# Linear attention with a squared-ReLU gate on one core: q rest formed with k and transposed by DMA, 1/den repeated through DRAM, g tiles on 128 rows, last tile in column parts

## Chip, cores and metric

One core of a Trainium2 chip. The metric is device microseconds of one execution; medians of several executions are quoted with their range. "Before" is the kernel without the change. Names of groups such as "k", "h", "g" are explained below.

## The reference

bf16 inputs, one batch of S = 2048 tokens, D = 448 features, F = 1792 hidden features, H = 16 heads of Dh = 28.

```python
def attention(x):                       # x here is LN(x)
    q, k, v = split(x @ wqkv)           # 16 heads of 28 each
    phi = lambda t: where(t > 0, t + 1, exp(t)) + 1e-6
    kv  = einsum("bhsd,bhse->bhde", phi(k), v)
    z   = einsum("bhsd->bhd", phi(k))
    num = einsum("bhqd,bhde->bhqe", phi(q), kv)
    den = einsum("bhqd,bhd->bhq", phi(q), z) + 1e-6
    return merge_heads(num / den) @ wo

def mlp(x):                             # again LN(x)
    r = relu(x @ w1 + b1)
    return (r * r) @ w2 + b2

xn  = layernorm(x)
out = x + attention(xn) * silu(mlp(xn))
```

## The kernel before

The kernel orders its own instructions. A Python description adds operations with the tiles that they read and write; the order on TensorE (PE) and on the DMA-issuing SyncE (SP) is the order of the description, and a list scheduler reorders ScalarE (ACT), VectorE (DVE) and GpSimd (POOL).

The stages on PE are: **k** (16 tiles of 128 tokens), **q** (4 groups of 512 tokens by 3 blocks of 128 features), **q rest** (the last 64 of 448 q features), **h** (x·w_1), then the **token sums** A = xnᵀ·phi(k), from which two small products (**fold_wv**, **fold_wo**) make one 448x448 matrix msb; **z** and **den**; the **spread** of 1/den over features; **g** (h²·w_2, 16 tiles), and **s** (scaled phi(q)·msb, 16 tiles). K = 448 is 3.5 times 128, so most products run as two 64-row halves of the array at once, one for each of two tiles, in seven half steps. `phase` is the function that interleaves two tiles; `half[0]` and `half[1]` are rows 0 to 63 and 64 to 127.

k and q rest, before:

```python
def kk(si):
    b = Buf("K")
    def mm(e, h, c, start, stop):
        return e.matmul(ps(b)[:, 0:D], xT[half[h], c, si*P:(si+1)*P], w_qkv[half[h], c, D:2*D], ...)
    return Acc(b, [("xT", si)] + wnames("wk"), mm, lambda: phi(b, pk[:, si, :], ("pk", si), P, D), D)

def q_rest(pair):                       # 64 features, two groups of 512 tokens side by side in columns
    b = Buf("Q")
    def mm(e, h, c, start, stop):
        for i in (0, 1):
            g = 2*pair + i
            last = e.matmul(ps(b)[half[i], 0:512], w_qkv[half[h], c, 384:448],
                            xT[half[h], c, g*512:(g+1)*512], ...)
        return last
    ...
```

1/den, before: `rden` is a [128, 512] tile with one row for each head and token group. A selector matrix `ehd` repeats each row over the 28 features of its head, into PSUM, and DVE multiplies phi(q) by it:

```python
def spread(*what):                      # seven calls, two (group, feature block) each
    bufs = [Buf("RB") for _ in what]
    def f(e, _):
        for h, (g, r) in enumerate(what):
            w = ehd[half[h], g % 2, r*P:(r+1)*P] if r < 3 else ehr[half[h], :, :]
            last = e.matmul(ps(bufs[h])[:, 0:512], w, rden[half[h], :], start=True, stop=True)
        return last
    add("pe", f, ["rden", "ehd", "ehr"], bufs, 0.22)
    for (g, r), b in zip(what, bufs):   # 14 products on DVE, one operand in PSUM
        ...  e.tensor_tensor(out=sl, in0=sl, in1=ps(b)[:, 0:512], op=ALU.mult)
```

The order after the last h group, and the last tile, before (cut):

```python
r0, r1 = q_rest(0), q_rest(1)
phase((r0, K4), (r1, K4)); phase((r1, K3), (r0, K3))
token_sum(0); z_heads(); token_sum(1); den(); token_sum(2); token_sum(3); fold_wv()
...                                     # six h tiles and the first g pairs, with spread() between them
gd = gg(15, True)                       # last g tile, a 64-row half beside s tiles, bias by matmul
...
ss_columns(15, 0)                       # last s tile: two halves of 224 columns,
ss_columns(15, 1)                       # each 3 matmuls on 128 rows and 1 on 64
```

Of the kernel before, what the change touches and what calls it, by code (L numbers as in the profile page):

```python
# [9 lines left out]
P = 128  # L10
# [270 lines left out]
def bass_recurrent_scan__linear_attn_block__dense_activation_squared_relu__prompt_kernel(  # L281
    nc, A_x, A_wqkv, A_wo, B_x, B_w1, B_b1, B_w2, B_b2, out
):
    with ExitStack() as es:
# [11 lines left out]
        c64 = sb("c64", [P, P], bf)  # L296
        ones = sb("ones", [P, 1], bf)
        ehd = sb("ehd", [P, 2, D], bf)
        ehr = sb("ehr", [P, 2, 64], bf)
# [15 lines left out]
        pqR = sb("pqR", [P, 2, 512], bf)  # L315
        pk = sb("pk", [P, NT, D], bf)
        zacc = sb("zacc", [P, D], f32)
        zb = sb("zb", [P, D], bf)
        at = sb("at", [P, 4, D], bf)
        r2 = sb("r2", [P, NF, S], bf)  # L320
        kvm = sb("kvm", [P, 4, D], bf)
        msb = sb("msb", [P, 4, D], bf)
        zsb = sb("zsb", [P, 5, 32], bf)
# [3 lines left out]
        obuf = sb("obuf", [P, 8, D], bf)  # L327
        pbank = [es.enter_context(nc.psum_tensor(f"pb{i}", [P, 512], f32)) for i in range(PSUM_BANKS)]

# [36 lines left out]
        pool(lambda e, _: e.memset(ones[:, :], 1.0), ["ones"], dur=0.1)  # L366
        pool(lambda e, _: e.memset(zmask[:, :, :], 1.0), ["zmask"])
# [5 lines left out]
        def late_constants(gate):  # L373
            pool(lambda e, _: e.memset(kvm[:, :, :], 0.0), ["kvm"], gate, dur=1.6)
            pool(lambda e, _: e.memset(hmask[:, :], 1.0), ["hmask"], gate)
            band("hmask", hmask[:, :].rearrange("p (b j) -> p b j", b=HC), [[-DH, HC], [0, DH]], 0)
            pool(lambda e, _: e.memset(ehd[:, :, :], 0.0), ["ehd"], gate, dur=0.85)  # L377
            for g in range(NG):
                ev = ehd[:, g % 2, :].rearrange("p (b j) -> p b j", b=NH)
                pool(  # L380
                    lambda e, _, g=g, ev=ev: e.affine_select(
                        out=ev, in_=ev, pattern=[[-1, NH], [0, DH]], compare_op=ALU.not_equal, fill=1.0,
                        base=-32 * g, channel_multiplier=1,
                    ),
                    ["ehd"], ["ehd"], dur=0.7,
                )
            pool(lambda e, _: e.tensor_copy(ehr[:, :, :], ehd[:, :, 384:448]), ["ehr"], ["ehd"])
            pool(lambda e, _: e.memset(c64[:, :], 1.0 / 64), ["c64"], gate)
# [35 lines left out]
        load_k("sp", w_qkv, A_wqkv, "wk", D, 2 * D)  # L424
# [5 lines left out]
        load_k("sp", w_qkv, A_wqkv, "wq", 0, D)  # L430
# [143 lines left out]
        def phi(buf, slot, tile, rows, n):  # L574

            act_d = 0.544 if n == D else 0.6
            add(
                "act", lambda e, _: e.activation(out=slot, in_=ps(buf)[0:rows, 0:n], func=AF.Exp), [buf, "actw"],  # L578
                [tile], act_d,
            )  # L580
            add(
                "dve",
                lambda e, _: e.tensor_scalar(
                    out=slot, in0=slot, scalar1=1.0, scalar2=1e-6, op0=ALU.min, op1=ALU.add
                ),
                [tile], [tile], 0.25,
            )
            add(
                "dve",
                lambda e, _: e.scalar_tensor_tensor(  # L590
                    out=slot, in0=ps(buf)[0:rows, 0:n], scalar=1.0 + 1e-6, in1=slot, op0=ALU.add, op1=ALU.max
                ),
                [tile, buf], [tile], 0.625 if n == D else 0.69,
            )

        def kk(si):
            b = Buf("K")

            def mm(e, h, c, start, stop):
                return e.matmul(  # L600
                    ps(b)[:, 0:D], xT[half[h], c, si * P : (si + 1) * P], w_qkv[half[h], c, D : 2 * D], start=start,
                    stop=stop,
                )

            return Acc(b, [("xT", si)] + wnames("wk"), mm, lambda: phi(b, pk[:, si, :], ("pk", si), P, D), D)

        def zsum(i):
# [5 lines left out]
                    out=o[:, :], in0=pk[:, 0, :] if i == 1 else zacc[:, :], in1=pk[:, i, :], op=ALU.add  # L613
                ),
                [("pk", i), ("pk", 0) if i == 1 else "zacc"], ["zb" if i == NT - 1 else "zacc"], 0.55,
            )

        def qq(g, m):
# [9 lines left out]
            return Acc(b, reads, mm, lambda: phi(b, pqT[:, m, g * 512 : (g + 1) * 512], ("pq", g, m), P, 512), 512)  # L628

        def q_rest(pair):  # L630

            b = Buf("Q")

            def mm(e, h, c, start, stop):
                for i in (0, 1):
                    g = 2 * pair + i
                    last = e.matmul(  # L637
                        ps(b)[half[i], 0:512], w_qkv[half[h], c, 384:448], xT[half[h], c, g * 512 : (g + 1) * 512],
                        start=start, stop=stop,
                    )  # L640
                return last

            reads = [("xT", 8 * pair + i) for i in range(8)] + wnames("wq")
            return Acc(b, reads, mm, lambda: phi(b, pqR[:, pair, :], ("pqr", pair), P, 512), 512)
# [29 lines left out]
        def token_sum(c):  # L674
# [3 lines left out]
            def f(e, _):  # L678
                last = None
                for si in range(NT):  # L680
                    if c < 3:
                        last = e.matmul(  # L682
                            ps(b)[:, 0:D], xn[:, si, c * P : (c + 1) * P], pk[:, si, :], start=(si == 0),
                            stop=(si == NT - 1),
                        )
                    else:
                        r = slice(64 * (si % 2), 64 * (si % 2) + 64)
                        last = e.matmul(  # L688
                            ps(b)[r, 0:D], xn[:, si, 384:448], pk[:, si, :], start=(si < 2), stop=(si >= NT - 2)
# [14 lines left out]
        def z_heads():  # L704
# [3 lines left out]
            def f(e, _):  # L708
                for r in range(3):
                    e.matmul(  # L710
                        ps(b)[:, r : r + 1], zb[:, r * P : (r + 1) * P], ones[:, :], start=(r == 0), stop=True,
                        skip_group_check=True,
                    )
                for col in (3, 4):
                    for i in (0, 1):
                        last = e.matmul(
                            ps(b)[half[i], col : col + 1], zb[:, 384:448], ones[:, :], start=False, stop=True,
                            skip_group_check=True,
                        )
                return last  # L720
# [10 lines left out]
        def fold_wv():  # L731
# [20 lines left out]
            def mask(e, _):  # L752
                o = kvm[0:PD, 0, 0:PD]
                o = bass.AP(tensor=o.tensor, offset=o.offset, ap=[o.ap[0], [D + PD, 4], [1, PD]])
# [5 lines left out]
            add("dve", mask, [b, "hmask"], ["kvm"], 0.65)  # L760

        def fold_wo(r):
# [3 lines left out]
            def f(e, _):  # L766
                if r == 3:
                    for i in (0, 1):
                        last = e.matmul(
                            ps(b)[half[i], 0:D], kvm[0:PD, 3, 384:448], w_o[0:PD, 3, :], start=True, stop=True  # L770
                        )
                    return last
# [17 lines left out]
            to(msb[:, r, :], half[2], [("msb", r)])  # L790
        denb = Buf("DEN")

        def den():
            def f(e, _):
                last = None
                for c in range(4):
                    for g in range(NG):
                        if c < 3:
                            z, q = zsb[:, c, :], pqT[:, c, g * 512 : (g + 1) * 512]
                        else:  # L800
                            z, q = zsb[:, 3 + g % 2, :], pqR[:, g // 2, :]
                        last = e.matmul(  # L802
                            ps(denb)[32 * g : 32 * g + 32, 0:512], z, q, start=(c == 0), stop=(c == 3)
# [4 lines left out]
                "pe", f, ["zsb", ("pqr", 0), ("pqr", 1)] + [("pq", g, c) for g in range(NG) for c in range(3)], [denb],  # L808
                4 * 0.24,
# [11 lines left out]
        def spread(*what):  # L821


            bufs = [Buf("RB") for _ in what]

            def f(e, _):
                for h, (g, r) in enumerate(what):
                    w = ehd[half[h], g % 2, r * P : (r + 1) * P] if r < 3 else ehr[half[h], :, :]
                    last = e.matmul(ps(bufs[h])[:, 0:512], w, rden[half[h], :], start=True, stop=True)  # L829
                return last  # L830

            add("pe", f, ["rden", "ehd", "ehr"], bufs, 0.22)
            for (g, r), b in zip(what, bufs):
                sl = pqT[:, r, g * 512 : (g + 1) * 512] if r < 3 else pqR[:, g // 2, :]
                name = ("pq", g, r) if r < 3 else ("pqr", g // 2)
                add(
                    "dve",
                    lambda e, _, sl=sl, b=b: e.tensor_tensor(out=sl, in0=sl, in1=ps(b)[:, 0:512], op=ALU.mult),  # L838
                    [b, name], [name], 0.68,
                )  # L840

        first_g = [True]

        def gg(si, last=False):

            b = Buf("G")

            def mm(e, h, fi, start, stop):
                if fi == NF:
                    return e.matmul(ps(b)[:, 0:D], c64[half[h], :], b2b[half[h], :], start=start, stop=stop)  # L850
                return e.matmul(  # L851
                    ps(b)[:, 0:D], r2[half[h], fi, si * P : (si + 1) * P], w_2[half[h], fi, :], start=start, stop=stop
                )

            def out():
                gs = gbuf[:, si % 8, :]
                if not last:
                    add(
                        "dve", lambda e, _: e.tensor_tensor(out=gs, in0=ps(b)[:, 0:D], in1=b2b[:, :], op=ALU.add),  # L859
                        [b, "b2b"], [("g", si % 8)], 0.624,  # L860
                    )
                if first_g[0]:
                    first_g[0] = False
                    add(
# [258 lines left out]
```

## Time and profile before

| | before |
|---|---|
| median of 3 runs | 147.03 us (147.02 to 147.06) |
| span of the profiled run | 145.9 us |
| PE busy | 140.8 us (97%) |
| DVE, ACT, POOL busy | 97.2, 79.8, 21.2 us |
| first h matmul starts | 9.80 us |
| first h to last matmul start | 132.88 us |
| last matmul start to end of span | 3.18 us |

The last rows are worked out from the matmul start times in the trace.

The head of the page of before: busy microseconds, share of the span and instruction count of each engine.

```profile
span 145.9 us, 3228 instructions
...
PE 140.8 (97%) x1330; PEld 69.1 (47%) x1330; DVE 97.2 (67%) x224; ACT 79.8 (55%) x154; POOL 21.2 (15%) x39
```

A row of the table of stretches of before, 80 to 90 us: for each stretch, its length and the busy time of each engine, then the granted clock, the DMA share and GB/s.

```profile
core 0: us, PE busy (x) PEld busy (x) DVE busy (x) ACT busy (x) POOL busy (x), PEclk, DMA share, GB/s
...
80.00:90.00 10.00, 10.00 (x98) 4.86 (x96) 6.41 (x12) 4.43 (x8) 0.00 (x0) 1.00 0.01 2
```

PE is busy 10.00 of 10 us, DVE and ACT less; the same holds for every stretch from 10 to 140 us, but for 9.93 at 60 to 70. So a microsecond of PE work removed is a microsecond of time, as long as no new wait replaces it. What PE does between 64 and 100 us is in the chain of waits, cut here to that stretch (start, duration, what; "x16" is a run of 16 matmuls):

```profile
66.22 1.02 PE pb L637 x16
67.28 0.84 PE pb L637 x12
68.12 3.13 PE pb L682 x16
...
81.39 0.97 PE pb L650 x8
82.36 0.22 PE pb L829 x2
82.57 1.51 PE pb L650 x14
```

L637 is q rest, L682 the token sums, L650 h, L829 the spread. They follow each other with hardly a gap. The groups of instructions that the change touches, with count, busy us, mean ns of one, and idle time before them with what ended it:

```profile
L838 DVE TENSOR_TENSOR pqT<-pqT,pb 128x512 bf16<-128x512 bf16 x12 | 7.7, 683 | 3.1 <-PE pb L829 3.1
...
L583 DVE TENSOR_SCALAR pk<-pk 128x448 bf16<-128x448 bf16 x16 | 4.3, 272 | 5.6 <-ACT pk L578 5.6
...
L829 PE MATMUL pb<-rden,ehd 64*128 64x512 bf16 x12 | 2.3, 376 | 0.0
...
L637 PE MATMUL pb<-xT,w_qkv 64*64 64x512 bf16 x28 | 1.9, 383 | 0.1
```

A matmul's duration here (376 ns) is not its pace: matmuls are pipelined, and two halves of the array run side by side. Paces are read from start to start: a pair of 64-row matmuls takes 0.189 us at 448 columns and 0.216 us at 512; one 128-row matmul of 448 columns takes 0.1895 us. The Trainium skill ("TensorE: Matmul & The Clock Gate", section "Back-to-back issue gap") gives N/2.4 + 2.5 ns as the gap of an isolated warm matmul, which is 189.2 ns for 448 columns, and calls it too high for streams of wide matmuls. In this trace the streams keep to the formula (the last section has the numbers). So a product that fills 128 rows and the same product as two halves beside another tile's cost the same.

The end of before in the timeline (start, duration of the run, engine, line, operation; in brackets the idle time before and what ended it; ACTq and SPq are the sequencers of ACT and SP, here issuing a DMA):

```profile
141.42 0.35 PE L850 MATMUL pb<-b2b,c 64*128 64x448 bf16 x1
...
141.70 0.46 PE L929 MATMUL pb<-msb,pqT 128*128 128x224 bf16 x3
...
142.09 0.27 PE L931 MATMUL pb<-msb,pqR 64*128 64x224 bf16 x1
...
142.29 0.46 PE L929 MATMUL pb<-msb,pqT 128*128 128x224 bf16 x3
...
142.69 0.27 PE L931 MATMUL pb<-msb,pqR 64*128 64x224 bf16 x1
143.06 0.39 DVE L888 TENSOR_TENSOR obuf<-pb,gbuf 128x224 bf16<-128x224 f32 x1 [0.21 <-PE pb L931]
143.37 0.68 DVE L898 TENSOR_TENSOR obuf<-obuf,x_tok 128x448 bf16<-128x448 bf16 x2
144.08 0.37 ACTq L395 DMA_DIRECT2D out_dram<-obuf  x1
```

### The profile page before, as it was taken

What the parts mean: (1) busy time and instruction counts of PE and PEld (TensorE: products, weight loads), DVE (VectorE), ACT (ScalarE), POOL (GpSimd) and SP (SyncE); (2) the same over time, 40 slices, a digit from 0 to 9 for tenths busy, and PEclk for the clock granted to TensorE, in tenths of its full rate; (3) what the DMA queues carried; (4) which work ended last, traced back from release to release, by engine and by line L of the source; (5) the groups of instructions that cost most, each with busy time, mean ns of one, the idle gap of its engine ahead of it and who ended that gap; (6) DMA issues with size and microseconds to landing.
All of it is one profiled execution on the core that took longest, in us unless ns stands there. A gap on an engine that the chain in (4) does not pass through costs nothing.

```text
span 145.9 us, 3228 instructions
## 1 busy us (share of the span) xinstructions
PE 140.8 (97%) x1330; PEld 69.1 (47%) x1330; DVE 97.2 (67%) x224; ACT 79.8 (55%) x154; POOL 21.2 (15%) x39
## 2 busy tenths in 40 slices
PE   6899999999999999999999999999999999999992
PEld 2344446654444446443544534545555555555440
DVE  0979688888968995999996584983061432504484
ACT  3657799888888888889797191623030311301310
POOL 6000000000000000007900000000040505053241
PEclk9999999999999999999999999999999999999998
DMA  4998769995301100000000000000001011020122
GB/s 119 315 314 232 79 166 330 315 222 114 65 11 36 36 4 0 0 0 4 0 0 0 4 0 0 7 0 0 0 4 63 31 36 47 15 65 2 63 94 94
DMA packets 15513, 10.54 MB, mean 72 GB/s; under 512 B 7244, under 2 KB 15116, under 8 KB 15500
## 3 DMA queue, kind: packets, MB, share of 16 engines
q1 hardware_dynamic: 15040, 9.89, 27.4%
q10 hardware_dynamic: 460, 0.46, 1.0%
q8 instruction: 10, 0.16, 0.5%
q14 instruction: 3, 0.02, 0.1%
HBM read 6.94 MB, written 1.84 MB: 60 GB/s over the span
## 4 chain that ended last, share of the span: by engine, by line
PE 93%; DMA 3%; DVE 2%; ACTq 0%; issue 0%; DVEq 0%
PE pb L650 29%; PE pb L851 29%; PE pb L600 7%; PE pb L911 7%; PE pb L682 6%; PE pb L622 6%; DMA x_tok<-in_A_x_dram 3%; PE pb L637 1%; PE pb L688 1%; PE pb L829 1%; PE pb L774 1%; PE pb L740 1%; PE pb L802 1%; PE pb L929 1%; PE pb L489 1%; DVE st L446 0%
## 5 line engine op out<-in xcount | busy, mean ns | idle before, releaser
L650 PE MATMUL pb<-xT,w 64*128 64x512 bf16 x392 | 51.6, 376 | 0.1
L851 PE MATMUL pb<-w,r 64*128 64x448 bf16 x448 | 48.2, 349 | 0.0
L659 ACT ACTIVATE r<-pb,b1f 128x512 bf16<-128x512 f32 x56 | 34.9, 688 | 9.0 <-PE pb L650 8.9
L851 PEld LDWEIGHTS pb<-w,r 64*128 64x128 bf16 x448 | 22.8, 94 | 21.0 <-PE pb L851 0.6
L650 PEld LDWEIGHTS pb<-xT,w 64*128 64x128 bf16 x392 | 21.7, 94 | 21.7 <-ACT r L659 0.6
L869 ACT ACTIVATE gbuf<-gbuf 128x448 bf16<-128x448 bf16 x15 | 8.3, 576 | 35.7 <-DVE gbuf L859 35.7
L859 DVE TENSOR_TENSOR gbuf<-pb,b2b 128x448 bf16<-128x448 f32 x15 | 8.7, 619 | 25.4 <-PE pb L851 25.4
L898 POOL TENSOR_TENSOR obuf<-obuf,x_tok 128x448 bf16<-128x448 bf16 x12 | 12.2, 1030 | 57.4 <-DVE obuf L888 57.4
L600 PE MATMUL pb<-w_qkv,xT 64*128 64x448 bf16 (+1 forms) x106 | 16.0, 350 | 0.0
L622 PE MATMUL pb<-xT,w_qkv 64*128 64x512 bf16 x84 | 15.6, 376 | 0.0
L667 DVE TENSOR_TENSOR r<-r 128x512 bf16<-128x512 bf16 x37 | 13.7, 439 | 0.0
L911 PE MATMUL pb<-msb,pqT 64*128 64x448 bf16 x90 | 13.6, 349 | 0.0
L668 ACT ACTIVATE r<-r 128x512 bf16<-128x512 bf16 x19 | 11.3, 633 | 0.0
L446 DVE BATCH_NORM_STATS2 st<-x_tok 128x6 f32<-128x448 bf16 x16 | 9.4, 611 | 2.6 <-DMA x_tok<-in_A_x_dram 2.6
L888 DVE TENSOR_TENSOR obuf<-pb,gbuf 128x448 bf16<-128x448 f32 (+1 forms) x17 | 9.6, 590 | 2.2 <-PE pb L851 1.7
L578 ACT ACTIVATE pk<-pb 128x448 bf16<-128x448 f32 x16 | 8.1, 540 | 3.6 <-PE pb L600 2.9
L590 DVE SCALAR_TENSOR_TENSOR pk<-pb,pk 128x448 bf16<-128x448 f32 x16 | 9.8, 622 | 0.4
L377 POOL MEMSET ehd<- 128x896 bf16 x1 | 0.8, 844 | 63.1 <-DVE zb L612 63.1
L838 DVE TENSOR_TENSOR pqT<-pqT,pb 128x512 bf16<-128x512 bf16 x12 | 7.7, 683 | 3.1 <-PE pb L829 3.1
L682 PE MATMUL pb<-pk,xn 128*128 128x448 bf16 x48 | 9.6, 353 | 0.0
L600 PEld LDWEIGHTS pb<-w_qkv,xT 64*128 64x128 bf16 (+1 forms) x106 | 6.8, 94 | 5.1 <-DVE xT L499 0.4
L622 PEld LDWEIGHTS pb<-xT,w_qkv 64*128 64x128 bf16 x84 | 6.3, 94 | 4.3
(90 smaller groups left out, 116.9 us busy)
## 6 DMA issues: line engine op xcount, KB each, us to landing
out_dram<-obuf SPq DMA_DIRECT2D x15, 112.0 KB, 1.7
w<-in_B_w_dram SPq DMA_DIRECT2D x1, 1568.0 KB, 9.6
x_tok<-in_A_x_dram SPq DMA_DIRECT2D x3, 448.0 KB, 4.2
w_qkv<-in_A_wqkv_dram SPq DMA_DIRECT2D x3, 336.0 KB, 5.0
w<-in_B_w_dram SPq DMA_DIRECT2D x2, 384.0 KB, 4.7
w<-in_B_w_dram SPq DMA_DIRECT2D x1, 576.0 KB, 5.9
w_o<-in_A_wo_dram SPq DMA_DIRECT2D x1, 392.0 KB, 10.8
w_qkv<-in_A_wqkv_dram SPq DMA_DIRECT2D x6, 56.0 KB, 4.6
```

What stands on the lines that cost most here:

```text
L590: lambda e, _: e.scalar_tensor_tensor(out=slot, in0=ps(buf)[0:rows, 0:n], scalar=1.0 + 1e-6, in1=slot, op0=ALU.add, op1=ALU.max),
L600: return e.matmul(ps(b)[:, 0:D], xT[half[h], c, si * P : (si + 1) * P], w_qkv[half[h], c, D : 2 * D], start=start, stop=stop,)
L622: return e.matmul(ps(b)[:, 0:512], w_qkv[half[h], c, m * P : (m + 1) * P], xT[half[h], c, g * 512 : (g + 1) * 512], start=start, stop=stop,)
L650: return e.matmul(ps(b)[:, 0:512], w_1[half[h], c, fi * P : (fi + 1) * P], xT[half[h], c, g * 512 : (g + 1) * 512], start=start, stop=stop,)
L659: lambda e, _: e.activation(out=slot, in_=ps(b)[:, 0:512], func=AF.Relu, bias=b1f[:, fi : fi + 1]),
L667: return e.tensor_tensor(out=slot, in0=slot, in1=slot, op=ALU.mult)
L668: return e.activation(out=slot, in_=slot, func=AF.Square)
L682: last = e.matmul(ps(b)[:, 0:D], xn[:, si, c * P : (c + 1) * P], pk[:, si, :], start=(si == 0), stop=(si == NT - 1),)
L851: return e.matmul(ps(b)[:, 0:D], r2[half[h], fi, si * P : (si + 1) * P], w_2[half[h], fi, :], start=start, stop=stop)
L888: lambda e, _: e.tensor_tensor(out=obuf[:, si % 8, c], in0=ps(b)[:, 0:n], in1=gbuf[:, si % 8, c], op=ALU.mult),
L898: eng, lambda e, _: e.tensor_tensor(out=ob, in0=ob, in1=x_tok[:, si, :], op=ALU.add),
L911: return e.matmul(ps(b)[:, 0:D], q, msb[half[h], k, :], start=start, stop=stop)
```

## The change

The intent is to take matmul work off PE, in four parts:

1. **q rest with k.** The last 64 q features lie before k in w_qkv, so one 512-wide matmul over columns 384:896 forms both. They come out with tokens on partitions, so eight small DMA transposes turn phi(q rest) to features on partitions.
2. **1/den through DRAM.** `rden` is stored to DRAM and read back by 22 DMAs whose source has stride 0 over the features of a head, so each row lands on up to 28 partitions, 1.8 MB in all. DVE multiplies from SBUF, one product for each token group and one for its rest. The spread matmuls go.
3. **g tiles 0 to 3, 14 and 15 on 128 rows**, placed around the token sums to cover the round trip; the rest of h is moved ahead of them.
4. **Last tile in 256 + 192 columns**, all on 128 rows (the rest is padded with zero rows), so that less is left to do after the last matmul. z takes 4 matmuls for 7.

```diff
 def kk(si):
-    ps(b)[:, 0:D], xT[half[h], c, si * P : (si + 1) * P], w_qkv[half[h], c, D : 2 * D], ...
+    ps(b)[:, 0:512], xT[half[h], c, si * P : (si + 1) * P], w_qkv[half[h], c, 384 : 2 * D], ...
-def q_rest(pair): ...
+def rest_transpose(pair):
+    add("sp", lambda e, _: e.dma_start_transpose(
+        out=pqR[:, pair * P : (pair + 1) * P], in_=qk[:, pair, 0:P]), ...)
-def spread(*what): ...
+def scale_q():
+    dma("sp", rows_d[:, :], rden[:, :], ["rows"], P * 1024, ["rden"])
+    ...                                  # and the two parities of rden to tiles_d, from ACT
+    def replicate(eng, dst, src, h, step, n, name, reads):
+        src = bass.AP(tensor=src.tensor, offset=src.offset + h * n,
+                      ap=[[0, dst.shape[0]], [step, NG], [1, n]])
+        dma(eng, dst.rearrange("p (g t) -> p g t", g=NG), src, [name], ...)
+    ...                                  # 22 calls, alternately on SP and ACT; dst overlays xT
+    for g in range(NG):
+        ...  e.tensor_tensor(out=pqT[sl], in0=pqT[sl], in1=rb[sl], op=ALU.mult)      # 128x3x512
+        ...  e.tensor_tensor(out=pqR[:, c], in0=pqR[:, c], in1=rbR[:, c], op=ALU.mult)  # 128x256
 ... (order)
-r0, r1 = q_rest(0), q_rest(1)
-phase((r0, K4), (r1, K4)); phase((r1, K3), (r0, K3))
-token_sum(0); z_heads(); token_sum(1); den(); token_sum(2); token_sum(3); fold_wv()
-...
+for i in range(3): phase((tail_h[i], K4), (tail_h[i + 3], K4))
+for i in range(3): phase((tail_h[i + 3], K3), (tail_h[i], K3))
+full(gg(0)); full(gg(1)); z_heads(); token_sum(0); den(); open_gates(); scale_q()
+token_sum(3); token_sum(1); token_sum(2); full(gg(2)); fold_wv(); full(gg(3))
+for r in range(4): fold_wo(r)
+...                                      # g pairs 4 to 13 with s pairs, as 64-row halves
+full(gg(14))
+KS = (3, 0, 1, 2); ca, cb = slice(0, 256), slice(256, D)
+full(ss(14), KS, ["msz"])
+full(gg(15, ca));                  full(ss(15, ca, eng="dve", end=False), KS, ["msz"])
+full(gg(15, cb, True), range(NF + 1)); full(ss(15, cb, eng="dve", end=False), KS, ["msz"])
+store(15, [ca, cb], "act")
```

## The prediction

> **What bounds the kernel.** TensorE. The page gives PE 140.8 of 145.9 us (97%), the chain of waits is 93% PE, and in the table of stretches PE is busy 10.0 of every 10 us from 10 us on (9.93 in 60-70). DVE (67%) and ACT (55%) are off the chain, though both are 80-95% busy between 10 and 80 us. From the first h matmul (9.8 us) to the last matmul (about 143 us) PE never waits, so the change is worth the PE columns it removes, plus any new wait.
>
> **PE time, from the timeline.** Pace of a pair of 64-row matmuls: 448 wide 0.189 us, 512 wide 0.215 us. Full 128-row 448-wide matmuls (token sums: 16 in 3.04 us) 0.190 us. So g tiles on 128 rows gain nothing in themselves.
> - q rest leaves (66.14 to 68.05 us): -1.9.
> - k becomes 512 wide instead of 448: 98 half matmuls x 0.0129 plus the first pair: +1.45.
> - seven spread matmul pairs leave, 0.22 each: -1.5.
> - last s tile without 64/128-row switches (1.26 us for two column parts before), last fold of wo as one matmul (0.32 us before), z in 4 matmuls instead of 7, fewer den columns by parity: -0.5 in all.
> - last g in 256+192 columns, bias on 128 rows: about 0.
> PE sum: about -2.5 us.
>
> **Tail.** Before: last matmul, DVE multiply 0.39, two DVE adds 0.6 on 448 columns, store about 1.8. After: only 192 columns are left to multiply and add: about -0.3.
>
> **Moved off PE, costed for waits.** The chain den, Ln (0.69), Exp (0.63), store to DRAM (about 2, as output stores land in 1.7), then 22 read-backs, 1.8 MB, issued half by SP, half by ACT. Issues cost 0.4-0.6 us each in the trace, so 11 take about 6 us per queue; ACT's first ones stand behind the copy of token sum 1. The Trainium skill (DMA: Bandwidth & Descriptors, how many engines) lets 28 rows use 14 engines only; the trace has loads at 315 GB/s, so bandwidth (about 7 us) matters like issue. I estimate all landed 13-15 us after den. PE has 6.3 us of token sums, 1.6 for the rest, three stretches of 2.65 (g2, g3, first half of g4/g5), folds 2.3: about 18 us before the first s tile. DVE scales group 0 after its last fold copy, about 1.2 us (512-wide bf16 products pace at 0.36): slack under 1 us in DVE order, 3 us for the DMAs. Likely no wait, or a few tenths.
>
> DVE loses 14 products from PSUM (0.68 each, 9.6 us) and two q rest phis, and gains wider k phis (+0.08 each) and 4 x 1.2 us. The blocked layout of k should keep the fast mode of the in-place min/add: Trainium skill, VectorE: DVE Perf Modes, auto-detection, asks for step 1 and an even outermost dim (8 blocks). If not, DVE gains 0.3 us x 16.
>
> **Prediction: 144.3 us (143.3 to 146.4)**; faster by over 2% (under 144.1) 0.42, within 2% 0.52, slower 0.06.
>
> **Signs.** PE idle stays near 2 us; k line about 0.215 us a pair; no PE wait before the first s matmul; k min/add stays near 285 ns; group scale 0.9-1.0 us; eight small transposes land in about 3 us without delaying xT.
>
> **What would make it wrong.** Read-backs slower than estimated (the same few DRAM rows read 28 times, rows under 1 KB): PE waits at the first s tile, 1 to 5 us. ACT or DVE falling behind in 10-70 us, so PE waits for PSUM banks. Transposed q arriving late for den. Block-strided operands slowing matmuls. Otherwise the sum could be better by 0.5 us, if switches between 64- and 128-row tiles cost more than I count.

## More of the kernel before

After the last g matmul (L850, its bias) come two s column halves: three 128-row matmuls (L929), one 64-row matmul (L931), twice. A 224-column matmul needs 0.096 us, so three from 141.70 would be done at 141.99, but L931 starts at 142.09.

## The result, and the profile after

The changed kernel took 143.40 us (median of 4 runs, 143.13 to 143.75) beside 147.03 us of before (147.00 to 147.06). The ratio is 0.9755, with a 95% interval of 0.9732 to 0.9777. Ratios here are the mean time of one kernel's fast runs over that of the other's of the same rounds, so they are not quite the ratio of the medians quoted. The same file run again on another chip gave 0.9758.

The page of the changed kernel, the same two lines:

```profile
span 142.0 us, 3024 instructions
...
PE 137.8 (97%) x1215; PEld 67.4 (47%) x1215; DVE 91.3 (64%) x218; ACT 78.7 (55%) x151; POOL 23.4 (17%) x37
```

The span fell by 3.9 us, PE's busy time by 3.0 us, and PE is as full as before. The same stretch of the changed kernel:

```profile
80.00:90.00 10.00, 10.00 (x76) 5.00 (x75) 1.70 (x5) 4.23 (x6) 0.00 (x0) 1.00 0.37 93
```

Between 80 and 90 us DVE now works 1.70 us for 6.41 and the DMA engines are 37% busy for 1%. PE is full in both rows. The chain of waits of the changed kernel from 64 to 100 us:

```profile
63.99 7.77 PE pb L640 x72
71.76 5.40 PE pb L905 x28
...
77.25 3.05 PE pb L672 x16
...
80.62 0.65 PE pb L803 x12
...
82.91 6.16 PE pb L672 x32
...
95.19 1.14 PE pb L765 x6
...
96.51 2.76 PE pb L905 x28
99.27 0.75 PE pb L971 x7
```

L640 is h, L905 g, L672 token sums, L803 den, L765 fold_wo, L971 s. No q rest, no spread, and no wait before the first s matmul. The groups that answer to those shown of before:

```profile
L578 DVE TENSOR_SCALAR qk<-qk 128x512 bf16<-128x512 bf16 x16 | 4.6, 290 | 5.2 <-ACT qk L575 5.2
...
L866 DVE TENSOR_TENSOR pqT<-pqT,xT 128x1536 bf16<-128x1536 bf16 x4 | 3.8, 954 | 0.1
...
L872 DVE TENSOR_TENSOR pqR<-pqR,xT 128x256 bf16<-128x256 bf16 x4 | 1.1, 285 | 0.0
```

Fourteen products of 0.68 us from PSUM became four of 0.954 and four of 0.285 us from SBUF. The in-place min/add of k takes 290 ns at 512 columns, in eight strided blocks, against 272 ns at 448: its fast mode is kept. That agrees with the Trainium skill ("VectorE: DVE Perf Modes", section "What auto-detection actually checks"), which asks, for the fastest mode, for 16-bit elements at step 1, source and destination in SBUF, and outermost dimensions that are both even or equal.

The round trip of 1/den in the timeline of the changed kernel:

```profile
81.33 0.69 ACT L815 ACTIVATE lnd<-pb,eps 128x512 f32<-128x512 f32 x1 [1.54 <-PE pb L803]
82.04 0.63 ACT L819 ACTIVATE rden<-lnd 128x512 bf16<-128x512 f32 x1
82.70 0.35 SPq L393 DMA_DIRECT2D rows<-rden  x1
...
84.82 3.27 SPq L393 DMA_DIRECT2D xT<-rows  x8
...
90.24 1.18 ACTq L393 DMA_DIRECT2D xT<-tiles  x3
...
95.98 1.19 DVE L776 CAST msb<-pb 128x448 bf16<-128x448 f32 x2
...
97.32 0.96 DVE L866 TENSOR_TENSOR pqT<-pqT,xT 128x1536 bf16<-128x1536 bf16 x1
98.19 0.28 DVE L872 TENSOR_TENSOR pqR<-pqR,xT 128x256 bf16<-128x256 bf16 x1
...
99.11 0.35 PE L971 MATMUL pb<-msb,pqR 64*128 64x448 bf16 x2
```

Ln and Exp make rden by 82.67, the store is issued at 82.70, the first read-backs at 84.82, the last at 91.4. The last packet of them ended at 96.99 us by the trace's packet records, 0.3 us before DVE began to scale (97.32), and DVE's copies of the folded matrix (95.98, 1.19 us) had ended at 97.17. The rest of group 0 was scaled at 98.47, 0.6 us before the first s matmul (99.11).

The end of the changed kernel:

```profile
137.69 1.32 PE L905 MATMUL pb<-w,r 128*128 128x192 bf16 x14
...
139.01 0.41 PE L971 MATMUL pb<-msb,pqT 128*128 128x192 bf16 x3
...
139.52 0.36 DVE L941 TENSOR_TENSOR xn<-pb,gbuf 128x192 bf16<-128x192 f32 x1 [0.42 <-ACT gbuf L881]
139.92 0.26 DVE L950 TENSOR_TENSOR xn<-xn,x_tok 128x192 bf16<-128x192 bf16 x1
140.21 0.37 ACTq L393 DMA_DIRECT2D out_dram<-xn  x1
```

The last adds and the store wait for 192 columns instead of 224 and 448: the last matmul starts 2.83 us before the end, against 3.18.

### Where the 3.9 us came from

For this table every matmul is given the time from its start to the next matmul's start, summed over each group. It includes waits and hand-overs after a matmul. The last matmul has no next start and is left out; differences are of unrounded times.

| group | before, us | after, us | difference |
|---|---|---|---|
| k and q | 20.16 | 21.32 | +1.15 |
| q rest | 1.91 | 0 | -1.91 |
| spread | 1.53 | 0 | -1.53 |
| h | 42.37 | 42.41 | +0.04 |
| g with its bias | 42.68 | 42.52 | -0.16 |
| s | 10.96 | 10.81 | -0.16 |
| token sums | 10.93 | 10.82 | -0.11 |
| fold_wv, fold_wo | 2.60 | 2.25 | -0.36 |
| z | 0.31 | 0.11 | -0.20 |
| den | 0.98 | 0.98 | 0 |

The sum is -3.22 us; 0.11 us of the growth of k lies ahead of the first h matmul. So from first h to last matmul the time fell by 3.33 us, from 132.88 to 129.55; the tail fell by 0.35 and the head by 0.19. Together that is the 3.86 us of the span. That the head is an effect of the change is not shown: h starts between 9.57 and 10.09 us over the profiles of these kernels.

The first row understates what the wider k costs. In before, 0.12 us of late start at 13.6 us, after two k tiles, is charged to it. And of the 98 k half matmuls after the first h, 28 run beside a 512-wide half of q or h. The two halves do not wait for each other at every step. In before a 448-wide k half and a 512-wide h half start together at 22.71 us; at their fourth step the h half is already 0.08 us behind:

```profile
23.28 0.35 PE L600 MATMUL pb<-w_qkv,xT 64*128 64x448 bf16 x1
23.36 1.13 PE L650 MATMUL pb<-xT,w 64*128 64x512 bf16 x8
```

The lead evens out when k runs on the other half. By start-to-start times these 28 mixed pairs average 0.2025 us in before, half way between 0.189 and 0.216, and 0.216 in the changed kernel: +0.37 us. The 35 pairs of two k halves grew by 0.95 and the work ahead of the first h by 0.11, so the wider k costs 1.43 us in all. (q_alone below, whose k is 448 wide again, also has 0.2025 for mixed pairs.)

Several small gains (fold_wv, token sums, z, part of s) are not columns removed. Start-to-start times show what most of them are: whenever the next matmul uses another number of array rows or columns (64 to 128 rows, 128 to 64 or 32 columns), the next start comes 0.090 to 0.102 us later than the pace, in both kernels (one reads 0.120). Steps to 112 rows or columns show no such delay from 128-row g matmuls (91.55 and 95.03 us in the changed kernel). From 60 us on, before has 16 such changes, which add up to 1.54 us, the changed kernel 6 (0.56 us): 0.98 us less. In before three short matmuls of fold_wv, at 80.4, 81.0 and 81.1 us, also start 0.045 us late each, in the changed kernel none; why is not known. The Trainium skill ("TensorEngine Tiling (Array Packing)", section "Key Properties") says that changing the tiling mode drains TensorE; it gives no time, and here it is a tenth of a microsecond. A second cost is in before at 66.8 us: when both row halves swap their PSUM banks with nothing else between, as q rest's two phases do, the next start is 0.23 us late. Such a delay is called a hand-over here; that the banks are its cause is argued, not isolated.

### The profile page after: what moved, and what is told of

Same layout as the page of the kernel before. It is cut to its first block, busy times and chain, and to the rows that moved or that the text cites. A ratio compares the mean times of both kernels' runs of the same rounds, so it can differ in the third digit from the quotient of the medians.

```text
span 142.0 us, 3024 instructions
## 1 busy us (share of the span) xinstructions
PE 137.8 (97%) x1215; PEld 67.4 (47%) x1215; DVE 91.3 (64%) x218; ACT 78.7 (55%) x151; POOL 23.4 (17%) x37
## 4 chain that ended last, share of the span: by engine, by line
PE 93%; DVE 3%; DMA 2%; issue 0%; DVEq 0%
PE pb L905 30%; PE pb L640 30%; PE pb L597 8%; PE pb L971 8%; PE pb L672 6%; PE pb L628 6%; DMA x_tok<-in_A_x_dram 2%; DVE st L444 1%; PE pb L678 1%; PE pb L765 1%; PE pb L726 1%; PE pb L487 1%; PE pb L803 0%; DVE xn L466 0%; PE pb L488 0%; DVE xT L497 0%
## 5 line engine op out<-in xcount | busy, mean ns | idle before, releaser
L640 PE MATMUL pb<-xT,w 64*128 64x512 bf16 x392 | 50.8, 376 | 0.1
L905 PE MATMUL pb<-w,r 64*128 64x448 bf16 (+3 forms) x378 | 45.1, 343 | 0.0
L640 PEld LDWEIGHTS pb<-xT,w 64*128 64x128 bf16 x392 | 21.4, 94 | 23.3 <-ACT r L649 0.6
L905 PEld LDWEIGHTS pb<-w,r 64*128 64x128 bf16 (+1 forms) x378 | 22.9, 95 | 19.9 <-issue 1.2
L916 DVE TENSOR_TENSOR gbuf<-pb,b2b 128x448 bf16<-128x448 f32 (+1 forms) x16 | 9.3, 609 | 33.2 <-PE pb L905 33.2
L950 POOL TENSOR_TENSOR xn<-xn,x_tok 128x448 bf16<-128x448 bf16 x15 | 15.1, 1029 | 48.7 <-DVE xn L941 48.7
L597 PE MATMUL pb<-w_qkv,xT 64*128 64x512 bf16 (+1 forms) x106 | 17.6, 377 | 0.0
L971 PE MATMUL pb<-msb,pqT 64*128 64x448 bf16 (+3 forms) x93 | 11.2, 343 | 0.0
L575 ACT ACTIVATE qk<-pb 128x512 bf16<-128x512 f32 x16 | 9.0, 594 | 3.3 <-PE pb L597 2.7
L585 DVE SCALAR_TENSOR_TENSOR qk<-pb,qk 128x512 bf16<-128x512 f32 x16 | 10.7, 686 | 0.2
L941 DVE TENSOR_TENSOR xn<-pb,gbuf 128x448 bf16<-128x448 f32 (+2 forms) x17 | 9.3, 590 | 1.9 <-ACT gbuf L881 1.5
L672 PE MATMUL pb<-qk,xn 128*128 128x448 bf16 x48 | 9.4, 353 | 0.0
```

The costliest lines, as they stand in the source:

```text
L585: lambda e, _: e.scalar_tensor_tensor(out=slot, in0=src(), scalar=1.0 + 1e-6, in1=slot, op0=ALU.add, op1=ALU.max),
L597: return e.matmul(ps(b)[:, 0:512], xT[half[h], c, si * P : (si + 1) * P], w_qkv[half[h], c, 384 : 2 * D], start=start, stop=stop,)
L640: return e.matmul(ps(b)[:, 0:512], w_1[half[h], c, fi * P : (fi + 1) * P], xT[half[h], c, g * 512 : (g + 1) * 512], start=start, stop=stop,)
L672: last = e.matmul(ps(b)[:, 0:D], xn[:, si, c * P : (c + 1) * P], pk_of(si), start=(si == 0), stop=(si == NT - 1),)
L905: return e.matmul(ps(b)[:, 0:n], r2[half[h], fi, si * P : (si + 1) * P], w_2[half[h], fi, c], start=start, stop=stop)
L950: eng, lambda e, _: e.tensor_tensor(out=ob, in0=ob, in1=x_tok[:, si, c], op=ALU.add),
```

## The experiments

Eleven kernels ran. Differences to the changed kernel are differences of ratios times 147 us, against 0.9755 for the first call and 0.9758 for the second; for the third, which had no run of the changed kernel, 0.9755 again. The interval of each ratio reaches 0.25 to 0.36 us to either side, so a difference of two is uncertain by 0.4 to 0.5 us. What is said of smaller differences rests on the trace of one run of each kernel. The edits are against the changed kernel.

| run | median, us (range, runs) | ratio to before | 95% interval |
|---|---|---|---|
| q_alone | 144.13 (143.94 to 144.84, 6) | 0.9802 | 0.9779 to 0.9826 |
| spread_pe | 145.39 (145.21 to 145.52, 5) | 0.9874 | 0.9854 to 0.9893 |
| g_halves | 144.27 (144.01 to 144.51, 4) | 0.9798 | 0.9777 to 0.9820 |
| tail_whole | 144.00 (143.98 to 144.39, 4) | 0.9787 | 0.9767 to 0.9807 |
| after_again | 143.48 (143.24 to 143.87, 4) | 0.9758 | 0.9741 to 0.9775 |
| at_on_dve | 144.62 (144.24 to 145.03, 4) | 0.9833 | 0.9814 to 0.9853 |
| s_before_g | 144.43 (143.63 to 144.65, 6) | 0.9808 | 0.9784 to 0.9833 |
| distinct_rows (wrong) | 143.37 (1) | | |
| one_queue | 143.69 (143.44 to 144.08, 5) | 0.9767 | 0.9746 to 0.9789 |
| wide_rows | 143.52 (143.17 to 143.58, 4) | 0.9749 | 0.9729 to 0.9769 |
| more_switches | 143.77 (143.68 to 144.00, 4) | 0.9773 | 0.9755 to 0.9792 |

The medians of before were 147.17, 147.08 and 147.08 us.

### q_alone: part 1 undone

```diff
-ps(b)[:, 0:512], xT[...], w_qkv[half[h], c, 384 : 2 * D]
+ps(b)[:, 0:D],   xT[...], w_qkv[half[h], c, D : 2 * D]
+def q_rest(pair): ...        # as before, tokens ordered as the blocks of pqR
-rest_transpose(2 * g); rest_transpose(2 * g + 1)
+r0, r1 = q_rest(0), q_rest(1)
+phase((r0, K4), (r1, K4)); phase((r1, K3), (r0, K3))
 tail_h = [...]
```

> The changed kernel with q rest taken out of k again: k tiles 448 wide, q rest as 28 matmuls of 64x64 before the last h tiles, no small transposes. Main theory (the time is TensorE's columns): +1.9 us for q rest, -1.2 us for the narrower k, so about +0.7 us over the changed kernel (144.0 to 144.2 if that one is 143.4). Rival (the wide k also costs DVE and ACT time that TensorE waits for, so forming q rest with k gains nothing): the same time or less, and TensorE gaps in the 10-70 us stretch that are there in the changed kernel and gone here.

Measured: +0.7 us to the changed kernel. The q rest group costs 1.91 us again in the trace, and k and q fall back to about 20.1 us, leaving aside 0.79 us that PE waited for ACT at 13.3 us in the profiled run, one of the two slowest of the six (144.84; the median is 144.13). From first h to last matmul, without that wait, the time is +0.72 us. So part 1 is worth about 0.7 us: 2.0 us removed (q rest and the change of tile shape before it), 1.28 added after the first h. The eight transposes cost nothing visible.

### spread_pe: part 2 undone

```diff
-scale_q()                    # store, 22 read-backs, 8 products from SBUF
+spread((0, 0), (2, 0)); spread((0, 1), (2, 1)); ...   # between g and s phases, with spread_rest()
+                             # 14 products from PSUM; ehd built again on POOL
```

> The changed kernel with 1/den spread by seven pairs of matmuls again, placed among the half-row g tiles so that no switch between 64 and 128 rows is added; no DRAM round trip. Main theory: +1.5 us (7 x 0.215), about 144.9. Rival (the round trip, whose last packet lands at 97.0 us, 0.3 us before the first scaling, costs TensorE a wait in some runs): under +1.0, and its runs lie closer together than the 0.6 us spread of the changed kernel.

Measured: +1.75 us, the largest part. The spread groups take 1.74 us on PE (with two changes of tile shape), and one hand-over of 0.23 us at 103.8 us came from where I placed the first s phases next to each other. From first h to last matmul 131.53 us against 129.55 (+1.98). The rival, that the round trip gives back most of what the spread's removal gains, falls. Its side sign did come: these five runs lie within 0.31 us, those of the changed kernel within 0.62.

### g_halves: the first four g tiles as 64-row pairs

```diff
-full(gg(0)); full(gg(1))
+ga, gb, C = gg(0), gg(1), range(0, NF)
+phase((ga, C), (gb, C)); phase((gb, C), (ga, C))
 ...
-full(gg(2)); fold_wv(); full(gg(3))
+ga, gb = gg(2), gg(3)
+phase((ga, C), (gb, C)); fold_wv(); phase((gb, C), (ga, C))
```

> The changed kernel with its first four g tiles as pairs on 64 rows in place of 128 rows. Main theory (both forms pace at 0.189 us for 448 columns; only a switch costs about 0.1 us): within 0.3 us of the changed kernel; g groups sum to 42.5 to 42.8 us of TensorE time. Rival (128 rows are faster in themselves): 0.5 us or more slower.

Measured: +0.6 us, more than the 0.3 that I had allowed. The pace of the pairs is the same (0.189 us for two halves, 0.1895 us for one full matmul). But the kernel has 10 changes of tile shape instead of 6, about 0.38 us, and a hand-over of 0.23 us at 74.1 us, where the halves of the first two g tiles swap banks with nothing between. From first h to last matmul it takes 130.25 us (+0.69). So 128 rows gain nothing in pace; they spare changes and hand-overs. That was the first sign that these are what the prediction missed.

### tail_whole: part 4's column parts undone

```diff
-full(gg(15, ca)); full(ss(15, ca, ...)); full(gg(15, cb, True), range(NF + 1)); full(ss(15, cb, ...))
-store(15, [ca, cb], "act")
+full(gg(15, slice(0, D), True), range(NF + 1)); full(ss(15, slice(0, D), ...)); store(15, [slice(0, D)], "act")
```

> The changed kernel with its last tile in one piece of 448 columns, still on 128 rows. Main theory (the tail after the last matmul is what column parts shorten): TensorE itself 0.1 us less, DVE multiply 0.62 instead of 0.36 and add 0.38 instead of 0.26, silu 0.58 now ahead of the multiply: +0.3 us, from 0.2 to 0.5. Rival (the parts are worth nothing because the store or ACT ends it): within 0.1 us.

Measured: +0.5 us; the last matmul starts 3.27 us before the end instead of 2.83 (+0.44). The profiled run, the slowest of its four, also had a late start of h (10.09 us) and a PE wait of 0.25 us at the first s tile. The column parts are worth about what the tail shows.

### after_again: the changed kernel once more

No edit.

> The changed kernel unaltered, to pair with the next two on one chip. 143.1 to 143.9 us, in two groups 0.4 to 0.5 us apart; theory: the groups come from the wait for the second x tile at the start (0.38 us after the two narrow warming matmuls in one profile, 0.86 in another of the same order of work), which no part of the change touches.

0.9758. The last packet of the read-backs ended at 97.27 us, scaling began at 97.61, no PE wait. Its own runs span 143.24 to 143.87: differences of half a microsecond between single runs mean nothing. Two groups of times do not stand out in four runs, so the theory of the second x tile is neither shown nor refuted.

### at_on_dve: a try to start ACT's read-backs earlier

In the changed kernel ACT copies token sums (L690) between its DMA issues, so the last read-backs are issued late. Here DVE does all those copies.

```diff
-add("dve", ev, [b], [("at", c)], 0.63, alts=[("act", 0.55)])
+add("dve", ev, [b], [("at", c)], 0.63)
```

> The changed kernel with all four copies of the token sums on DVE, so that ACT's share of the read-backs isn't held behind them. Theory (the round trip's end, 97.0 us, is set by ACT issuing its last six at 89.1 to 91.4 us, behind a copy that waits for TensorE): issues end near 89.5, the last packet lands near 95, and the first scaling still starts near 97.3, behind the copies of the fold; the time is the same or up to 0.2 us less. Rival (the DMA engines' rate sets it): landing stays at 96.5 to 97.

The theory fell: +1.1 us. Issues did end earlier (90.66 us instead of 91.42), but the last packet ended later, at 98.79 instead of 96.99. In the timeline of this kernel:

```profile
99.09 0.96 DVE L866 TENSOR_TENSOR pqT<-pqT,xT 128x1536 bf16<-128x1536 bf16 x1 [1.69 <-DMA xT<-rows]
...
100.55 0.36 PE L971 MATMUL pb<-msb,pqR 64*128 64x448 bf16 x2 [1.07 <-DVE pqR L872]
```

DVE waited 1.69 us for the DMA, and PE 1.07 us for DVE (1.23 us by start-to-start). The median of the 1 KB packets was 91 ns here and 68 ns in the changed kernel. Earlier issue is not earlier landing, and the read-backs have no slack to spare. That the edit made them land later is not shown: tail_whole and s_before_g change nothing ahead of the first s tile, and their last packets landed at 98.40 and 98.44 us.

### s_before_g: the last s columns ahead of the last g columns

```diff
+full(sa, KS, ["msz"], out=False); full(sz, KS, ["msz"], out=False)
 full(gg(15, ca))
-full(ss(15, ca, eng="dve", end=False), KS, ["msz"])
+sa.out()
 full(gg(15, cb, True), range(NF + 1))
-full(ss(15, cb, eng="dve", end=False), KS, ["msz"])
+sz.out()
```

> The changed kernel with the s matmuls of the last tile's two column parts moved ahead of that tile's g matmuls. Theory (in the changed kernel DVE's last multiply waits 0.4 us for the silu, while TensorE spends 0.33 us on s after the last g matmul): the same work, with the last silu 0.33 us earlier: 0.25 to 0.4 us less than the changed kernel of the same call. Rival (the tail is set by the store or by an earlier tile): within 0.1 us.

The theory fell: +0.7 us. The time from the start of the last g's bias matmul to the end is 3.19 us, as in the changed kernel (3.16): the 0.33 us of s columns after it had already run beside the SiLU of the last g, so moving them ahead only delays the last g. The profiled run had, besides, 0.53 us of PE waiting at the first s tile, with the last packet at 98.44 us.

### distinct_rows: the same traffic from different DRAM rows

The prediction feared that reading the same few DRAM rows 28 times is slow. Here each partition reads another row of w1; the result is wrong (relative error about 1,077), bytes and packets are the same.

```diff
-ap=[[0, dst.shape[0]], [step, NG], [1, n]]           # of rows_d or tiles_d
+ap=[[F, dst.shape[0]], [320, NG], [1, n]]            # of B_w1
```

> Wrong result on purpose: the 22 read-backs keep size, shape, order and waits, but read 28 different rows of w1 each in place of one row 28 times. Theory (reading the same DRAM row 28 times isn't what holds them; issue order is): last packet within 0.7 us of the changed kernel's 97.0, the same time. Rival (repeated rows are slow, the risk that the prediction named): last packet 2 us or more earlier.

143.37 us, last packet 96.92 us (96.99 in the changed kernel). Repeated rows are not what limits the read-backs.

### one_queue: all read-backs issued by SP

```diff
-("sp", "act")[len(names) % 2], rb[...]
+"sp", rb[...]
-("sp", "act")[len(rest) % 2], rbR[...]
+"sp", rbR[...]
```

> The changed kernel with all 22 read-backs issued by SP. In the changed kernel 150 to 180 KB land per us while one queue alone is at work (packets 45 ns) and about 150 while both are (packets 70 to 110 ns); with both at work all along the last packet came at 98.8 us. Theory (the two queues' packets slow each other, so one queue is no slower than two): the last packet at 97 us or earlier though 22 issues of 0.4 us end near 94; no wait at the first s tile; time within 0.3 us of the changed kernel's 143.4. Rival (issue counts: a single issuer is the limit): last packet after 98, a wait of 0.5 us or more at the first s tile.

Time +0.2 us, within the noise. Issuing ended two microseconds later (93.55 us), and the last packet landed at 97.14, as before. The Trainium skill ("DMA: Bandwidth & Descriptors", section "Issuing engines are not separate DMA queues") says that issuing from several engines saves only the time of issuing; the runs agree. PE waited 0.3 us at the first s tile, for another reason:

```profile
97.51 1.83 DVE L866 TENSOR_TENSOR pqT<-pqT,xT 128x1536 bf16<-128x1536 bf16 x2
99.26 0.49 DVE L872 TENSOR_TENSOR pqR<-pqR,xT 128x256 bf16<-128x256 bf16 x2
...
99.60 0.36 PE L971 MATMUL pb<-msb,pqR 64*128 64x448 bf16 x2
```

The scheduler put two group products (1.83 us) ahead of the rest that the first s tile needs first. (The "about 150" KB per us of the expectation is rough: with both queues at work, packets of 112 to 241 KB started in each us from 88 to 95 in the changed kernel.)

### wide_rows: the same bytes in packets of 4 KB

```diff
-rows_d = nc.dram_tensor("rows", [P, 512], ...)       # a head's four groups 32 rows apart
+rows_d = nc.dram_tensor("rows", [16, 2048], ...)     # a head's four groups in one row
-ap=[[0, dst.shape[0]], [step, NG], [1, n]]
+ap=[[0, dst.shape[0]], [1, n]]                       # n = 2048, for the 128-row part
```

> The changed kernel with 1/den kept in DRAM as 16 rows of 2048 instead of 64 of 512, so that a read-back row is one run of 4 KB, not four of 1 KB (the small half for q rest unchanged). Theory (the number of packets, not the bytes, sets the round trip; the first s tile waits for it in some runs, 0.25 to 1.2 us in three of the profiles): last packet before 95 us, no wait at the first s tile, runs at the low end, 143.1 to 143.5. Rival (bytes or the write side set it): last packet still at 96.5 or later, the time unchanged.

The 1,536 packets of 1 KB became 384 of 4 KB, and the last packet ended at 96.28 us: 0.7 us earlier, not the 2 us or more that the theory of packet cost asked for. From first issue to last packet it took 11.0 us, against 12.0 to 13.1 in seven profiles whose read-backs are as in the changed kernel. That theory falls as stated: a quarter of the large packets saves about 1 us of 12, and what sets the rest stays open. The time did not move (0.9749), as the changed kernel does not wait there.

### more_switches: four more changes of tile shape, nothing else

```diff
-for i in range(3): phase((tail_h[i + 3], K3), (tail_h[i], K3))
-full(gg(0)); full(gg(1))
+full(gg(0))
+phase((tail_h[3], K3), (tail_h[0], K3))
+full(gg(1))
+for i in (1, 2): phase((tail_h[i + 3], K3), (tail_h[i], K3))
```

> The changed kernel with its first two g tiles (128 rows) put between the closing steps of the last h tiles (64 rows): the same work, four more changes between 64 and 128 rows. Theory (each change of the tile's rows or columns costs TensorE 0.09 to 0.10 us; the kernel before had ten more of them than the changed one): 0.35 to 0.4 us more TensorE time between the first h and the last matmul. Rival (the 0.09 us gaps are how matmul ends are drawn, not time): no difference over 0.1 us.

From first h to last matmul the time is 129.98 us, +0.43, with no other wait on PE: 0.1 us for each of the four changes, as the theory said. In the timeline of this kernel:

```profile
69.71 2.82 PE L905 MATMUL pb<-w,r 128*128 128x448 bf16 x14
72.46 0.82 PE L640 MATMUL pb<-xT,w 64*128 64x512 bf16 x6
73.22 2.82 PE L905 MATMUL pb<-w,r 128*128 128x448 bf16 x14
```

Fourteen g matmuls (L905) at 0.1895 us would end their turn at 72.36, but h (L640) starts at 72.46; its three pairs at 0.216 us would end theirs at 73.11, but g starts at 73.22. By the ratio it is +0.26 us, with an interval as wide as itself; the trace decides here. (This order also delays two h pairs by a few microseconds, which nothing waited for.)

## Why the prediction was right

The time, 143.4 us, lies inside the range of 143.3 to 146.4, but 0.1 us above its lower end and 0.9 us below the value of 144.3; and "within 2%" had been given more (0.52) than "faster by over 2%" (0.42), which came. The mechanism was right: PE work removed, no new wait. Its terms compare so:

- **PE bounds the kernel; the change is worth the PE time that it removes.** Right: PE is 97% busy in both, and the table of groups adds up to the span's gain.
- **q rest -1.9, spread -1.5.** -1.91 and -1.53; spread_pe confirms the second by undoing it.
- **k 512 wide: +1.45.** Right: +1.43 by pairs. The k and q row shows only +1.15, as it holds the late start of before (0.12) and as part of the cost of mixed pairs is charged to h or q.
- **"-0.5 in all" for the last s tile, fold of wo, z and den.** -0.49 for those four (-0.16, -0.13, -0.20, 0). The gain in den was not there: 0.98 us in both. fold_wv (-0.23), token sums (-0.11) and g (-0.16) were not on the list: another 0.5. This is the mis-sized term, as the prediction's last sentence allowed: the changes of tile shape. Six of the ten that left stand in groups that had been counted (last tile, fold_wo, z, q rest). Four did not, one each in h, g, token sums and fold_wv: 0.37 us. g_halves pointed to it and more_switches shows what one costs.
- **PE sum about -2.5.** -3.33 from first h to last matmul, -3.22 with the growth of k ahead of it. Of the missing 0.8 us, the four changes are 0.37, the late matmuls of fold_wv 0.14, the late start of before at 13.6 us 0.12 ("PE never waits" was not quite so), and the bias by matmul over 192 columns for 448 about 0.1. The late start is of one profile and belongs to no part of the change.
- **Tail -0.3.** -0.35; tail_whole gives +0.44 for undoing the column parts.
- **Round trip: landed 13 to 15 us after den; likely no wait, or a few tenths.** It landed 15.7 us after den (81.27 to 96.99), with no wait in two profiles of the changed kernel. But "3 us for the DMAs" was wrong: DVE began 0.33 us after the last packet in the profiled run, and not all of that is slack: in s_before_g and at_on_dve, where DVE stood waiting for the last packet, it began 0.14 and 0.30 us after it. In DVE order slack was about 0.6 us, where "under 1" was right. So no wait was in part luck: PE in tail_whole and s_before_g, whose edits change nothing ahead of the first s tile, waited 0.25 and 0.53 us there, so some executions of the changed kernel may wait as well. The skill's statement about 14 engines for 28 rows, on which that estimate leaned, was not tested: no record here shows an engine.
- **Signs.** Group scale 0.954 us (0.9 to 1.0 said), k min/add 290 ns (near 285), no PE wait, transposes at 2.4 us median (about 3): all as said.

What stays open: what sets the landing of the read-backs, and why packets slow down in some orders (at_on_dve). About 1.8 MB took 12 us, half the 315 GB/s of the loads at the start. Repeated rows, the number of queues and, for the most part, the packet count are not it, as far as one profile each can show; the write side and the number of DMA engines in use were not tested. Nor is the spread of half a microsecond or more between runs of one kernel settled: the first h start varies between 9.57 and 10.09 us over the profiles of these kernels, and the last packet between 96.3 and 98.8. No version beats the changed kernel by more than the noise.

## What to carry to other kernels

When one engine is full, count what leaves it, but look at start-to-start times: each change of tile shape between 64 and 128 rows, or from 128 to 64 or 32 columns, cost a tenth of a microsecond here that no busy table shows, so keep equal shapes together. A broadcast that only feeds VectorE can go through DRAM with stride 0 if, as here, 16 us of other work cover it, and the faster SBUF operands come as a bonus. Widening a 64-row matmul costs its share even where it runs beside a wider one: the halves drift apart and catch up later (0.2025 us a mixed pair, not 0.216).

## What the Trainium skill lacked or had wrong

- "TensorEngine Tiling (Array Packing)" says that a change of tiling mode drains TensorE, without a time. Here it costs 0.09 to 0.10 us for each change between 64 and 128 rows or to 64 or 32 columns (four more: +0.43 us).
- "PSUM — Partial Sum Buffer" (section "PSUM bank collisions raise a hardware error") quotes that different row tiles cannot access the same bank at once and leaves the synchronization to software. Where two row halves swapped banks with nothing between, the next matmul started 0.23 us late, in all four places (before at 66.8 us, q_alone at 67.4, spread_pe at 103.8, g_halves at 74.1). That the bank is the cause is argued, not isolated.
- "TensorE: Matmul & The Clock Gate" gives a sustained 131 ns for a 512-column matmul in a stream with weight loads, and calls its N/2.4 + 2.5 ns formula too high there. The runs show 189.5 ns at 448 columns in streams of 14 or more, and 215.9 ns for pairs of 64-row matmuls at 512, which is the formula, and no faster.
- "DMA: Bandwidth & Descriptors": no figure for read-backs with stride 0 over partitions. Here 1.8 MB in 22 of them took about 12 us from first issue to last packet, and repeated rows cost nothing that one look shows (last packet at 96.99 us, at 96.92 with distinct rows).
